# Batch 0 of k: two rows of w3 loaded ahead of it, its maximum taken by pairs of heads from PSUM, and a new order of the steps behind

## The chip, the cores and the metric

The kernel runs on one core of one Trainium2 chip. The metric is the device time of one execution in microseconds, lower is better. Each engine of the core (PE for matmuls, DVE and ACT and POOL for work on whole tiles, SP for DMA issues) takes its own instructions in the order in which the program gives them, and waits on semaphores for the others.

## The reference, cut to what matters

```python
# q, k, v: (8 batches, 8 heads, 576 tokens, 64)
q_s = exp(q - max(q, axis=-1));  q_s /= sum(q_s, axis=-1) + 1e-9     # over the 64 of a head
k_s = exp(k - max(k, axis=2));   k_s /= sum(k_s, axis=2) + 1e-9      # over the 576 tokens
kv  = einsum('bhsd,bhse->bhde', k_s, v)
x   = einsum('bhsd,bhde->bhse', q_s, kv)        # then as (8 * 576 tokens, 512)
h   = (x @ w1) * (x @ w2) @ w3                  # w1, w2: 512 x 1024, w3: 1024 x 1024
out = h @ w_out                                 # w_out: 1024 x 512, out: 4608 x 512
```

The maximum over k is taken over tokens, for each head and each of its 64 columns.

## The kernel before, in words

All work is cut into named steps. `Plan.add` registers a step with its engine and what it needs; the string `ORDER` is the order, written out by hand, in which the steps are emitted. So on each engine the steps stand in the order of `ORDER`, and a step that waits holds up all that stand behind it on that engine. A suffix (/A, /D, /P) chooses ACT, DVE or POOL where a step may run on more than one.

The steps that the opening of the kernel is made of, with their tiles in the profile:

- **Loads.** `q.0.0`, `q.0.1` and, from batch 2 on, all of q, k and v are issued by SP; all other loads (`w3.r` is row block r of w3, `wo` halves of w_out, `w1`, `w2` column blocks, `k.0.0` and `k.0.1` the two pairs of heads of batch 0, `v.0`, `k.1`, `q.1.x`, `v.1`) by POOL, in the order of `ORDER`. The load of q of batch 2 waits for the last block of w1 (`GATES`).
- **Fold of w3 and w_out into W3O.** For each row block ft: `w3t.ft` transposes it on PE into a PSUM bank (tile w3t), `w3T.ft` copies it to one of two buffers (tile aux), `pf.ft.0` and `pf.ft.1` multiply it with w_out on PE (tile pf), and `W3O.ft` scales the result out of PSUM. All `down` steps need all eight.
- **k of a batch b.** `kmx` takes the maximum over the nine blocks of tokens that lie in a partition's row (tile km); `cb` takes it across partitions and spreads it (tiles kmq, mx, mxe, cb); `ksub.b.hp` subtracts it for a pair of heads hp (tile k); `kexp.b.hp` takes the exponential (tile ek); `kv.b` multiplies with v (tile pkv) and `kv2.b` divides by the sum (tiles rc, kv). For batch 0, `kmx.0.hp` is one strided reduction for each pair of heads (`kmx_one`). For the other batches ACT first copies two blocks of all heads into PSUM (`kmi.b`, tile kmp), and DVE takes maxima of it with the other blocks, in place (`kmx_half`).
- **q of a batch.** `qmx`, `qsub`, `qexp`, `qsm`, `qeps`, `qrc`, `qn` make the softmax over a head's columns; `qt` and `qT` transpose it over PE (batch 0), `qd` by a DMA (the others).
- **x and the two layers.** `xm.b` and `xt.b` are the products of q and kv (tiles xm, xt), `xs`, `xts` scale them out of PSUM (tiles x, xtail); `up.1` and `up.0` multiply with w2 and w1 (tile pab), `bs` copies the first out (tile bsb), `ab` multiplies the two on DVE (tile ab), `down` multiplies with W3O (tile po), `os` and `st` bring the result out.
- **Sums for later chunks.** `ws` (from w1, w2) and `wt` (from W3O) are sums of weight blocks that later chunks use.

PSUM has eight banks; every step that makes a PSUM tile takes a bank that an earlier tile gave back (`w3T`, `W3O`, `xs`, `bs`, `ab` and so on give back). `zero` steps are matmuls of zeros that keep PE running at the start.

From about 80 us on (the step `up.0.2.0.1`) the order is the same in both kernels.

Of the kernel before, what the change touches and what calls it, by code (L numbers as in the profile page):

```python
# [109 lines left out]
st.0.3 qd.3.1 kmx.4.1 down.1.2 qrc.4.1 ab.2.0.4 down.1.3.0 up.0.2.0.6 up.1.2.0.7 up.0.2.0.7 qd.3.0 os.1.2/A down.1.3  # L110
bs.2.0.6/A qmx.5.0 ab.2.0.6 vc.3.0/A ksub.3.0/P kexp.3.0 st.1.2 qeps.4.0/A bs.2.0.7/A qn.4.1/P os.1.3/A qsub.5.0/P
qrc.4.0 qn.4.0/P cbt.4 cbx.4 kv.3 ab.2.0.7 qexp.5.0 down.2.0 kv2.3 xm.3.0 xs.3.0.1/A xs.3.0.0/A xm.3.1 xs.3.1.0/A xt.3
xts.3.1/A xts.3.0/A cb.4 ksub.4.1/P k.5 qmx.6.1 down.2.1 xs.3.1.1/D qsm.5.0 vc.4.1/A os.2.1/A ksub.4.0/P up.1.3.0.0
up.0.3.0.0 qmx.6.0 qsub.6.0/P bs.3.0.0/A ab.3.0.0 os.2.0/A qeps.5.0/A qrc.5.0 st.1.1 qmx.5.1 qsub.5.1/P up.1.3.0.1
up.0.3.0.1 up.1.3.0.2 up.0.3.0.2 bs.3.0.1/A qd.4.1 up.1.3.0.3 up.0.3.0.3 up.1.3.0.4 ab.3.0.1 v.5 kmi.5 kmx.5.0 kmx.5.1
cbt.5 st.2.1 kexp.4.0 vc.4.0/A kexp.4.1 kv.4 bs.3.0.2/A qsub.6.1/P kv2.4 bs.3.0.4/A up.0.3.0.4 ab.3.0.4 down.2.2
bs.3.0.3/A ab.3.0.2 qexp.5.1 qd.4.0 cbx.5 qsm.5.1 qexp.6.0 xm.4.1 xs.4.1.0/A xm.4.0 xs.4.0.1/A qn.5.0/P xs.4.0.0/A
up.1.3.0.5 ws.3.1/D up.0.3.0.5 up.1.3.0.6 up.0.3.0.6 v.6 qeps.5.1/A wt.4/D ws.4.0/D os.2.2/A wt.3/D ws.3.0/D qrc.5.1
qn.5.1/P qexp.6.1 cb.5 ksub.5.0/P bs.3.0.6/A ab.3.0.6 k.6 vc.5.0/A xs.4.1.1/A up.1.3.0.7 up.0.3.0.7 q.7 qsm.6.1
ab.3.0.3 bs.3.0.5/A vc.6.0/A up.1.4.0.0 ab.3.0.5 up.0.4.0.0 up.1.4.0.1 st.1.3 bs.3.0.7/A ksub.5.1/P up.0.4.0.1 qsm.6.0  # L120
kmi.6 bs.4.0.1/A bs.4.0.0/A kmx.6.0 st.2.0 vc.6.1/A down.2.3 qeps.6.1/A os.2.3/A qrc.6.1 kmx.6.1 up.1.4.0.2 qd.5.0
qn.6.1/P qeps.6.0/A qrc.6.0 qn.6.0/P up.0.4.0.2 ab.4.0.0 up.1.4.0.3 bs.4.0.2/A ab.4.0.2 up.0.4.0.3 up.1.4.0.4
up.0.4.0.4 cbt.6 kexp.5.0 bs.4.0.3/A vc.5.1/A qmx.7.0 qsub.7.0/P ab.4.0.3 cbx.6 up.1.4.0.5 ab.4.0.1 cb.6 up.0.4.0.5
ksub.6.1/P bs.4.0.4/A ab.4.0.4 ab.3.0.7 st.0.0 xt.4 kexp.5.1 kv.5 xts.4.0/A qexp.7.0 kv2.5 bs.4.0.5/A ab.4.0.5 dm.3.1
xts.4.1/D dm.3.2 de.3.1/A qd.5.1 xm.5.0 xm.5.1 xs.5.0.1/A xs.5.0.0/A qd.6.0 ad.3.1/D xs.5.1.0/A up.1.4.0.6 up.0.4.0.6
up.1.4.0.7 up.0.4.0.7 xs.5.1.1/A st.0.1 ksub.6.0/D kexp.6.0 ad.3.3/D bs.4.0.6/A dm.3.7 kexp.6.1 bs.4.0.7/A ws.2.1/D
ad.3.2/D dm.3.6 xd.5.3/D de.3.7/A ab.4.0.6 xt.5 ad.3.4/P qmx.7.1 ab.4.0.7 xts.5.1/D kv.6 xts.5.0/A dm.3.4 de.3.2/A
dm.3.5 de.3.4/A kv2.6 dc.3.3 qd.6.1 xm.6.1 xs.6.1.0/A qsub.7.1/P dc.3.1 xd.5.2/P xs.6.1.1/A qsm.7.0 um.5.2.1 um.5.1.1
ue.5.1.1/A ue.5.2.1/A xm.6.0 xd.5.4/D xt.6 xts.6.0/A ad.4.1/D dm.3.3 xts.6.1/A dc.3.2/A um.5.1.6 xd.5.1/D dc.3.4/D
ue.5.1.2/A k.7 xs.6.0.1/A ad.4.2/D um.5.2.6 ue.5.2.2/A ad.4.4/D um.5.1.7 ws.4.1/D um.5.2.7 ue.5.2.7/A um.5.0.7  # L130
um.5.1.5 ue.5.1.4/A ue.5.1.7/A ad.4.3/D um.5.2.2 uc.5.2.1 qeps.7.0/A um.5.0.1 xs.6.0.0/A um.5.2.4 uc.5.2.3 qrc.7.0
ue.5.0.7/A um.5.1.3 uc.5.1.4/P ab.5.1.1 ue.5.0.1/A um.5.2.5 ue.5.2.4/A um.5.1.2 uc.5.1.1 ab.5.2.0/P st.3.0 st.2.2
um.5.0.2 uc.5.0.1 um.5.0.4 um.5.0.6 ue.5.0.2/A uc.5.0.3 uc.5.2.4/P um.5.3.7 xd.6.3/P qn.7.0/P dm.4.1 kmi.7 kmx.7.0
um.5.3.1 ue.5.3.7/A um.5.1.4 uc.5.1.3 ab.5.1.0/P kmx.7.1 ue.5.3.1/A um.5.3.2 uc.5.3.1 de.4.1/A um.5.0.5 ue.5.0.4/A
uc.5.0.4/P um.5.3.6 xd.6.2/P ue.5.3.2/A dm.4.6 um.5.2.3 ab.5.2.1 um.6.0.1 qexp.7.1 qsm.7.1 cbt.7 um.5.3.5 ue.5.3.4/A
dm.4.2 xd.6.1/D dm.4.7 um.6.2.1 um.5.0.3 um.5.3.3 dc.4.1 ab.5.0.1 v.7 vc.7.1/A um.5.3.4 uc.5.3.3 uc.5.3.4/P ab.5.0.0/P
de.4.7/A dm.4.4 st.3.1 qeps.7.1/A qrc.7.1 ue.6.0.1/A ab.5.3.1 um.6.0.6 ab.5.3.0/P um.6.0.7 cbx.7 cb.7 de.4.2/A dc.4.3
xd.6.4/D ue.6.0.2/A ue.6.0.7/A ue.6.2.1/A dm.4.5 de.4.4/A dc.4.4/D um.6.0.5 ue.6.0.4/A uc.6.0.4/D st.4.1 um.6.1.1
ue.6.1.1/A um.6.2.7 ue.6.2.7/A dm.4.3 dc.4.2/A um.6.3.1 ue.6.3.1/A um.6.0.4 um.6.3.7 ue.6.3.7/A um.6.0.2 ksub.7.1/D
ksub.7.0/D qd.7.0 qn.7.1/P kexp.7.1 um.6.1.6 um.6.3.6 um.6.2.6 ue.6.2.2/A uc.6.0.3 uc.6.0.1 ab.6.0.0/P um.6.3.4  # L140
vc.7.0/A um.6.2.4 uc.6.2.3 um.6.0.3 ab.6.0.1 um.6.2.2 uc.6.2.1 um.6.1.2 uc.6.1.1 um.6.1.7 um.6.3.2 uc.6.3.1 ab.6.2.0/P
um.6.2.5 ue.6.3.2/A um.6.3.5 uc.6.3.3 kexp.7.0 ue.6.2.4/A ad.5.1/D uc.6.2.4/D dm.5.1 kv.7 ue.6.1.2/A ad.5.2/D
ue.6.3.4/A uc.6.3.4/P um.6.1.5 um.6.2.3 kv2.7 st.4.0 ue.6.1.7/A um.6.1.4 de.5.1/A uc.6.1.3 ab.6.2.1 dm.5.2 um.6.3.3
# [1039 lines left out]
```

## Time and profile before

| what | value |
|---|---|
| median of 3 runs | 227.33 us (227.28 to 227.34) |
| the profiled execution | 227.57 us, its span 225.8 us |
| PE busy | 219.3 us (97%) |
| DVE busy | 203.9 us (90%) |
| ACT busy | 161.6 us (72%) |
| POOL busy | 141.1 us (62%) |
| read from and written to HBM | 38.80 MB, 9.44 MB |

The span is the time from the program's first to its last instruction; the execution's own time is somewhat longer. A row of the timeline has the start, the duration, the engine, the line, the operation, the tiles (out<-in) with their shapes, how many instructions the row merges, and in brackets the engine's idle time ahead of it with what ended it. The ends of matmuls are modelled, so a short wait of PE can stand in a row as a longer duration.

### The profile page before, as it was taken

The numbers are of one execution on the slowest core, as the hardware profiler recorded it, in microseconds if no ns is written. First come the engines' busy times: TensorE is split into PE (matmuls) and PEld (weight loads), VectorE is DVE, ScalarE is ACT, GpSimd is POOL, SyncE is SP. The second block draws the span as 40 slices with busy tenths as digits, with TensorE's granted clock in tenths as the row PEclk, the third lists the DMA queues.
The fourth block names the chain that finished last, engine by engine and source line by source line (L and its number), as shares of the span: only waits on it lengthen the run. The fifth ranks groups of instructions, "written<-read, shape, count | busy, mean of one in ns | idle before, by whom it ended". The sixth has DMA issues, their size and how long they took to land.

```text
span 225.8 us, 5662 instructions
## 1 busy us (share of the span) xinstructions
PE 219.3 (97%) x2250; PEld 150.6 (67%) x2250; DVE 203.9 (90%) x363; ACT 161.6 (72%) x280; POOL 141.1 (62%) x96
## 2 busy tenths in 40 slices
...
GB/s 222 214 273 248 294 227 251 367 387 300 277 276 369 388 324 357 187 312 280 385 164 296 22 134 212 128 221 96 32 200 64 3 107 34 3 124 157 89 145 139
DMA packets 38042, 46.89 MB, mean 208 GB/s; under 512 B 18048, under 2 KB 21504, under 8 KB 38016
## 3 DMA queue, kind: packets, MB, share of 16 engines
...
q8 instruction: 17, 0.28, 0.5%
...
HBM read 38.80 MB, written 9.44 MB: 214 GB/s over the span
## 4 chain that ended last, share of the span: by engine, by line
PE 67%; DMA 20%; DVE 8%; ACT 2%; POOL 1%; issue 1%; POOLq 0%; ACTq 0%; SPq 0%; DVEq 0%
PE pab L809 19%; PE uA L904 12%; PE dA L945 8%; DMA w1sb<-in_moe_w_dram 8%; PE uB L904 6%; PE po L842 6%; DMA w<-in_moe_w_dram 5%; DMA wosb<-in_moe_w_out_dram 5%; PE dB L945 4%; DMA q<-in_q_dram 3%; PE uC L904 3%; PE po L857 3%; PE dC L945 2%; DVE qm L547 2%; PE pkv L501 2%; DVE qr L579 2%
## 5 line engine op out<-in xcount | busy, mean ns | idle before, releaser
L809 PE MATMUL pab<-x,w2sb 128*128 128x256 f16 (+1 forms) x224 | 40.6, 318 | 0.0
L809 PE MATMUL pab<-x,w1sb 128*128 128x256 f16 (+1 forms) x224 | 40.6, 318 | 0.0
L597 POOL TENSOR_TENSOR en<-eq,qr 128x1024 f16<-128x1024 f16 (+1 forms) x14 | 29.7, 2126 | 8.3 <-DVE k L475 4.3
L809 PEld LDWEIGHTS <-w2sb 128*128 128x128 f16 x224 | 21.6, 98 | 13.4 <-issue 1.0
L809 PEld LDWEIGHTS <-w1sb 128*128 128x128 f16 x224 | 21.7, 98 | 13.0 <-issue 0.2
L553 POOL TENSOR_TENSOR q<-q,qm 128x1280 f32<-128x1280 f32 (+1 forms) x13 | 27.7, 2143 | 2.2 <-DVE qm L547 1.8
L475 POOL TENSOR_TENSOR k<-k,cb 128x1152 f32<-128x1152 f32 x10 | 26.2, 2626 | 2.5 <-DVE k L475 2.5
L904 PEld LDWEIGHTS <-w 128*128 128x128 f16 x256 | 25.0, 98 | 3.3
L834 DVE TENSOR_TENSOR ab<-pab,bsb 128x512 f16<-128x512 f32 x40 | 25.9, 672 | 0.2
L275 ACT CAST bsb<-pab 128x512 f16<-128x512 f32 x40 | 23.2, 594 | 3.8 <-PE pab L809 3.6
L561 ACT ACTIVATE eq<-q 128x1024 f16<-128x1024 f32 (+2 forms) x16 | 18.7, 1169 | 8.2 <-DVE q L553 7.6
L547 DVE TENSOR_REDUCE qm<-q 128x16 f32<-128x1024 f32 (+2 forms) x16 | 21.2, 1333 | 3.7 <-DMA q<-in_q_dram 3.7
L842 PE MATMUL po<-W3O,ab 128*128 128x512 f16 x96 | 22.7, 380 | 0.0
L579 DVE TENSOR_REDUCE qr<-eq 128x16 f32<-128x1024 f16 (+2 forms) x16 | 21.4, 1339 | 0.0
L483 ACT ACTIVATE ek<-k 128x1152 f16<-128x1152 f32 x16 | 18.8, 1172 | 3.3 <-DVE k L475 2.4
L279 ACT ACTIVATE x<-xm 128x512 f16<-128x512 f32 x30 | 16.4, 605 | 3.6 <-PE xm L649 1.9
L904 PE MATMUL uA<-v,w 128*128 128x256 f16 x128 | 17.9, 273 | 0.0
L275 ACT COPY v<-uA 128x512 f32<-128x512 f32 x24 | 14.1, 601 | 4.8 <-PE uA L904 4.3
L945 PEld LDWEIGHTS <-k 128*128 128x128 f16 x160 | 15.5, 98 | 2.1
L883 POOL TENSOR_TENSOR k<-ab,k 128x1024 f16<-128x1024 f16 x3 | 6.4, 2130 | 16.4 <-DVE bsb L883 10.0
L275 ACT CAST v<-v 128x1152 f16<-128x1152 f32 x14 | 16.3, 1170 | 0.0
L398 PE MATMUL pf<-wosb,aux 128*128 128x512 f16 x64 | 15.6, 379 | 0.4 <-DMA wosb<-in_moe_w_out_dram 0.4
(140 smaller groups left out, 464.7 us busy)
## 6 DMA issues: line engine op xcount, KB each, us to landing
...
```

The costliest lines, as they stand in the source:

```text
L275: return [(nc.scalar.copy if eng == "ACT" else engine[eng].tensor_copy)(out=out, in_=in_)]
L475: return [engine[eng].tensor_tensor(out=kb[:, two(hp), :, :], in0=kb[:, two(hp), :, :], in1=st["cb", b][:, two(hp), None, :].broadcast_to( ...
L483: nc.scalar.activation(out=st["ek", b][:, hp, :, :].rearrange("p j (i d) -> p i j d", i=2), in_=kb[:, two(hp), :, :], func=AF.Exp)
L547: dve.tensor_reduce(out=st["qm", b][:, hs, j], in_=qb[:, hs, j, :], axis=AX.X, op=ALU.max, **({"negate": True} if (b, p) in FEXP else {}))
L553: return [engine[eng].tensor_tensor(out=qb[:, hs, j, :], in0=qb[:, hs, j, :], in1=st["qm", b][:, hs, j, None].broadcast_to([P, nh, n, D]), ...
L579: dve.tensor_reduce(out=st["qr", b][(slice(None), *part(p))], in_=st["eq", b, p], axis=AX.X, op=ALU.add)
L597: return [engine[eng].tensor_tensor(out=st["en", b][:, j, hs, :].rearrange("p j h d -> p h j d"), in0=st["eq", b, p], in1=st["qr", b][:, h ...
L809: nc.tensor.matmul(st["p", one, c, sub, u][:, a * (t1 - t0):(a + 1) * (t1 - t0)], lhsT=w[:, ct, fb * P:(fb + 1) * P], rhs=x()[:, ct, t0:t1 ...
L834: dve.tensor_tensor(out=st["ab", c][:, nf * u:nf * u + nf, t0:t1], in0=cut(st["p", 0, c, sub, u]), in1=cut(st["bsb", c, sub, u]), op=ALU.mult)
L842: nc.tensor.matmul(st["po", c, tb], lhsT=st["ab", c][:, ft, tb * P:(tb + 1) * P], rhs=W3O[:, ft, :], start=(ft == 0), stop=(ft == N_FT - 1))
L904: nc.tensor.matmul(t[:, u, :], lhsT=w[:, k0 + kk, fb * P:(fb + 1) * P], rhs=r[:, kk, :], start=(p in (1, 2, 7) and u == 0 and kk == 0), st ...
L945: nc.tensor.matmul(t[:, i, :], lhsT=l[:, f, i * P:(i + 1) * P], rhs=r[:, f, :], start=(p in (1, 2, 7) and i == 0 and f == 0), stop=(i == 1 ...
```

## The change

`KM = [0]` gives batch 0 two new steps for each pair of heads hp in place of the strided reduction. `kmi.0.hp` (ACT) copies the first two blocks of tokens of the pair into a PSUM bank, as 2 x 128 columns; `kmx.0.hp` (DVE) takes the maximum of it with blocks 2 and 3, 4 and 5, 6 and 7 in place (three instructions of 256 columns), and then with block 8 and of the two halves (two of 128 columns). `ALOAD` is empty and so does nothing.

In `ORDER`, `w3.7` and `w3.5` are loaded ahead of `k.0.1` and `k.0.0`; the first 33 steps are the same, and from there to `up.0.2.0.1` the steps stand in a new order, thirteen of them on another engine (`qsub.1.0` and `ws.1.1` from DVE to POOL, `wt.2` from POOL to DVE, and moves between ACT and DVE).

```diff
-qt.0.0.4 qT.0.0.4/A wo.1 pf.3.1 zero.6/1 qsm.0.1 w3.6 w3t.6 qeps.0.1/A qrc.0.1 qT.0.0.0/D qn.0.1/D pf.4.1 W3O.4/D w3.0
-w3t.0 W3O.3/D w3T.6/A pf.6.0 qt.0.1.0 w3T.0/A qT.0.1.0/A qt.0.1.4 pf.6.1 qT.0.1.4/A W3O.6/A pf.0.0 k.0.1 kmx.0.1 k.0.0
-w3.7 w3t.7 w3T.7/A pf.0.1 w3.5 w3t.5 pf.7.0 pf.7.1 w3T.5/A pf.5.0 w3.1 w3.2 v.0 k.1 kmx.0.0 cb.0 ksub.0.0/D kexp.0.0
-w3t.1 w3T.1/D W3O.7/A ksub.0.1/D pf.5.1 w2.1 w2.0 w1.0 q.1.0 W3O.5/D w2.2 w3t.2 pf.1.0 kexp.0.1 pf.1.1 W3O.1/D w1.1
-kv.0.0 kv.0 kv2.0 w3T.2/A pf.2.0 kmi.1 kmx.1.0 xm.0.1 xt.0 xs.0.1.1/A xs.0.1.0/A xts.0.0/A xts.0.1/D pf.2.1 W3O.2/A
-xm.0.0 xs.0.0.1/A xs.0.0.0/A q.1.1 up.1.0.1.0 W3O.0/A wt.1/P up.1.0.1.1 up.1.0.0.1 up.1.0.0.0 bs.0.1.1/A up.0.0.0.0
-bs.0.0.1/A kmx.1.1 cb.1 bs.0.0.0/A qmx.1.0 up.0.0.0.1 up.0.0.1.0 qsub.1.0/D ksub.1.1/D ab.0.0.1 qexp.1.0 qsm.1.0
-up.1.0.0.3 bs.0.0.3/A up.0.0.1.1 ab.0.1.1 q.2 v.1 kexp.1.1 k.2 qeps.1.0/A ksub.1.0/P up.1.0.1.2 kexp.1.0 up.1.0.0.2
-qrc.1.0 bs.0.0.2/A qn.1.0/P up.0.0.0.3 up.0.0.0.2 ab.0.0.0 qmx.1.1 qd.1.0 qsub.1.1/P bs.0.1.0/A ab.0.0.3 up.1.0.1.3
-up.0.0.1.3 ab.0.0.2 k.3 ab.0.1.0 bs.0.1.3/A ab.0.1.3 ws.1.1/D up.0.0.1.2 bs.0.1.2/A ab.0.1.2 down.0.0.0 qmx.2.0
-down.0.0 down.0.1.0 down.0.1 vc.1.1/A vc.1.0/A qexp.1.1 qsm.1.1 qeps.1.1/A ws.1.0/P qsub.2.0/P kv.1.0 kv.1 q.3 kv2.1
-qexp.2.0 down.0.2.0 down.0.2 qrc.1.1 xm.1.0 qn.1.1/P qd.1.1 qmx.2.1 down.0.3.0 down.0.3 qsm.2.0 qeps.2.0/D kmi.2
-kmx.2.0 qsub.2.1/P xs.1.0.0/A v.2 xs.1.0.1/A up.1.1.0.0 bs.1.0.0/A os.0.2/A st.0.2 up.0.1.0.0 os.0.3/A qrc.2.0
-qn.2.0/P wt.2/P up.1.1.0.1 up.0.1.0.1 bs.1.0.1/A qexp.2.1 kmx.2.1 up.1.1.0.2 cb.2 bs.1.0.2/A ksub.2.0/P up.0.1.0.2
-up.1.1.0.3 os.0.0/A os.0.1/A xm.1.1 xs.1.1.1/A qsm.2.1 xs.1.1.0/D ab.1.0.1 qeps.2.1/A qrc.2.1 ab.1.0.0 bs.1.0.3/A
-up.0.1.0.3 up.1.1.1.0 up.0.1.1.0 up.1.1.1.1 qmx.3.1 up.0.1.1.1 ab.1.0.3 ab.1.0.2 bs.1.1.0/A up.1.1.1.2 up.0.1.1.2
-up.1.1.1.3 qn.2.1/P kexp.2.0 down.1.0.0 down.1.0 kmi.3 kmx.3.0 bs.1.1.1/A ab.1.1.1 vc.2.0/A qd.2.0 xt.1 bs.1.1.2/A
-ksub.2.1/P vc.2.1/A kmx.3.1 cbt.3 kexp.2.1 qsub.3.1/P xts.1.0/A ab.1.1.2 xts.1.1/A q.4 qexp.3.1 ws.2.0/P ab.1.1.0 kv.2
-kv2.2 down.1.1.0 down.1.1 qd.2.1 xm.2.1 qmx.3.0 qsub.3.0/P os.1.0/A bs.1.1.3/A xs.2.1.1/A qmx.4.1 qsub.4.1/P xm.2.0
-xs.2.0.1/A xt.2 qsm.3.1 xs.2.0.0/A xs.2.1.0/A cbx.3 xts.2.1/A v.3 down.1.2.0 up.0.1.1.3 up.1.2.0.0 bs.2.0.0/A qmx.4.0
-xts.2.0/D up.0.2.0.0 up.1.2.0.1 qsub.4.0/P up.0.2.0.1 up.1.2.0.2 k.4 v.4 qexp.3.0 cb.3 ksub.3.1/P qsm.3.0 os.1.1/A
...
+qt.0.0.4 qT.0.0.4/A wo.1 pf.3.1 w3.6 w3t.6 qT.0.0.0/A w3.0 w3.7 w3T.6/A pf.4.1 w3t.0 w3T.0/A w3.5 k.0.1 k.0.0 w3.1
+w3.2 kmi.0.1 qsm.0.1 qeps.0.1/D pf.6.0 qrc.0.1 qn.0.1/D pf.6.1 zero.6/1 W3O.3/D W3O.6/D qt.0.1.0 w3t.5 w3T.5/A w3t.7
+kmi.0.0 pf.0.0 pf.0.1 v.0 pf.5.0 kmx.0.1 qT.0.1.0/A w3T.7/A pf.5.1 W3O.5/A pf.7.0 kmx.0.0 cb.0 ksub.0.0/D w3t.2
+ksub.0.1/D w3T.2/A pf.7.1 kexp.0.0 qt.0.1.4 qT.0.1.4/D kexp.0.1 W3O.4/A pf.2.0 pf.2.1 w3t.1 w3T.1/D k.1 kv.0.0 kv.0
+kv2.0 W3O.0/A w2.1 w2.0 w1.0 q.1.0 w2.2 w1.1 q.2 pf.1.0 kmi.1 W3O.2/A W3O.7/A xm.0.0 xs.0.0.0/A xs.0.0.1/D xm.0.1
+xs.0.1.1/A q.1.1 xt.0 xts.0.1/D pf.1.1 up.1.0.0.1 up.1.0.0.0 kmx.1.0 xs.0.1.0/A up.1.0.1.0 bs.0.1.0/A v.1 xts.0.0/A
+up.1.0.1.1 up.0.0.1.1 up.0.0.1.0 W3O.1/D wt.1/P up.0.0.0.0 bs.0.1.1/A kmx.1.1 qmx.1.0 qsub.1.0/P bs.0.0.0/A up.1.0.0.2
+qexp.1.0 cb.1 bs.0.0.1/A ksub.1.1/D up.1.0.1.2 bs.0.0.2/A up.1.0.1.3 qsm.1.0 qeps.1.0/A bs.0.1.3/A ab.0.1.0 up.0.0.0.1
+kexp.1.1 ksub.1.0/P kexp.1.0 up.1.0.0.3 bs.0.0.3/A up.0.0.0.3 qrc.1.0 qn.1.0/P ab.0.1.1 qmx.1.1 ab.0.0.1 ab.0.0.0
+up.0.0.1.3 ab.0.1.3 up.0.0.0.2 ab.0.0.2 up.0.0.1.2 ab.0.0.3 k.2 bs.0.1.2/A ab.0.1.2 qmx.2.0 vc.1.1/A down.0.0.0
+down.0.0 vc.1.0/A down.0.1.0 qsub.1.1/P qexp.1.1 qsm.1.1 qeps.1.1/A qd.1.0 kv.1.0 kv.1 kv2.1 down.0.1 os.0.1/A v.2
+ws.1.1/P down.0.2.0 down.0.2 kmi.2 qsub.2.0/P qexp.2.0 xm.1.0 xs.1.0.0/A qrc.1.1 qmx.2.1 qn.1.1/P xs.1.0.1/A kmx.2.0
+qsm.2.0 q.3 kmx.2.1 os.0.0/A os.0.2/A qeps.2.0/A down.0.3.0 ws.1.0/P qrc.2.0 down.0.3 os.0.3/A up.1.1.0.0 up.0.1.0.0
+bs.1.0.0/A up.1.1.0.1 up.0.1.0.1 bs.1.0.1/A ab.1.0.0 up.1.1.0.2 up.0.1.0.2 up.1.1.0.3 qsub.2.1/P qexp.2.1 bs.1.0.2/A
+cb.2 bs.1.0.3/A qd.1.1 xm.1.1 xs.1.1.0/A xs.1.1.1/A xt.1 ab.1.0.1 qsm.2.1 qn.2.0/P up.0.1.0.3 down.1.0.0 qeps.2.1/A
+xts.1.0/A qmx.3.0 qrc.2.1 vc.2.1/A ab.1.0.2 k.3 ksub.2.0/P kmi.3 kexp.2.0 up.1.1.1.0 ab.1.0.3 qmx.3.1 up.0.1.1.0
+qn.2.1/P q.4 up.1.1.1.1 bs.1.1.1/A kmx.3.0 bs.1.1.0/A up.0.1.1.1 ab.1.1.0 kmx.3.1 vc.2.0/A qmx.4.0 st.0.2 xts.1.1/A
+up.1.1.1.2 ksub.2.1/P kexp.2.1 qd.2.0 up.0.1.1.2 up.1.1.1.3 bs.1.1.2/A ab.1.1.2 bs.1.1.3/A qsub.3.1/P qexp.3.1
+down.1.0 os.1.0/A kv.2 kv2.2 ab.1.1.1 qmx.4.1 down.1.1.0 down.1.1 qd.2.1 xm.2.0 xs.2.0.0/A xm.2.1 xs.2.1.1/A cbt.3
+xs.2.0.1/A xs.2.1.0/A xt.2 qsub.3.0/P xts.2.0/D qsub.4.0/P xts.2.1/D qsm.3.1 qsub.4.1/P down.1.2.0 cbx.3 up.0.1.1.3
+up.1.2.0.0 bs.2.0.0/A v.3 wt.2/D up.0.2.0.0 ws.2.0/P up.1.2.0.1 up.0.2.0.1 up.1.2.0.2 k.4 v.4 qexp.3.0 cb.3 ksub.3.1/P
...
@@
+    KM = [0]
+    ALOAD = []
@@
-            load((n, b), "SP")
+            load((n, b), "ACT" if (n, b) in ALOAD else "SP")
@@
+        def kmi_one(hp):
+            st["kmp", b, hp] = bank([P, 2, 2, D], F32, "kmp")
+            nc.scalar.copy(out=st["kmp", b, hp], in_=kb[:, two(hp), 0:2, :].rearrange("p h j d -> p j h d"))
+
+        def kmx_max(hp):
+            t = st["kmp", b, hp]
+            top = lambda out, in0, in1: dve.tensor_tensor(out=out, in0=in0, in1=in1, op=ALU.max)
+            for j in (2, 4, 6):
+                top(t, t, kb[:, two(hp), j:j + 2, :].rearrange("p h j d -> p j h d"))
+            if ("km", b) not in st:
+                st["km", b] = work.tile([P, HH, D], F32, tag="km", name="km")
+            m = st["km", b][:, two(hp), :]
+            top(m, t[:, 0], kb[:, two(hp), 8, :])
+            top(m, t[:, 1], m)
@@
             for hp in hps:
-                A(("kmx", b, hp), "DVE", lambda hp=hp: kmx_one(hp), [("k", b, hp)])
+                if b in KM:
+                    A(("kmi", b, hp), "ACT", lambda hp=hp: kmi_one(hp), [("k", b, hp)], takes="ps", kind="kmi1")
+                    A(("kmx", b, hp), "DVE", lambda hp=hp: kmx_max(hp), [("kmi", b, hp)], gives=[("kmi", b, hp)],
+                      kind="kmq")
+                else:
+                    A(("kmx", b, hp), "DVE", lambda hp=hp: kmx_one(hp), [("k", b, hp)])
```

113 lines of the change are left out of this document (57 added, 56 removed).

## The prediction

> **What bounds the kernel now.** I read the page first, then the chain, then the timelines of PE, POOL, DVE and ACT over the opening, since the order changes only up to about 80 us.
>
> ```profile
> PE 219.3 (97%) x2250; PEld 150.6 (67%) x2250; DVE 203.9 (90%) x363; ACT 161.6 (72%) x280; POOL 141.1 (62%) x96
> PE 67%; DMA 20%; DVE 8%; ACT 2%; POOL 1%; issue 1%; POOLq 0%; ACTq 0%; SPq 0%; DVEq 0%
> ```
>
> PE is busy 97% of the span, but the chain that ended last is PE for only 67%. The chain in order of time (start, us, what) says where the rest lies:
>
> ```profile
> 25.05 16.98 DMA w1sb<-in_moe_w_dram
> 42.10 7.75 DMA q<-in_q_dram
> 49.88 1.22 DVE qm L547
> ...
> 71.26 1.07 ACT ek L483
> 72.85 1.83 PE po L842 x8
> ```
>
> Up to 72.3 us the chain runs through the last weight load, q of batch 2 gated behind it, DVE and ACT; from 72.85 on it is PE alone. So two things must be followed: when the dense work of PE begins, and how much PE still waits between there and 72.85. The PE timeline (start, us; in brackets the idle time and who ended it):
>
> ```profile
> 22.63 0.71 PE L388 MATMUL w3t<-ident,w 128*128 128x128 f16 x8 [0.85 <-DMA w<-in_moe_w_dram]
> ...
> 30.15 0.48 PE L501 MATMUL pkv<-v,ek 64*64 64x64 f16 x36
> 30.56 0.38 PE L510 MATMUL pkv<-ones,ek 64*128 64x1 f16 x18
> ...
> 31.84 0.56 PE L649 MATMUL xm<-qT,kv 64*64 64x256 f16 x8
> 32.12 0.33 PE L649 MATMUL xt<-qT,kv 64*64 64x64 f16 x8
> 32.38 1.04 PE L398 MATMUL pf<-wosb,aux 128*128 128x512 f16 x4
> 33.35 0.41 PE L649 MATMUL xm<-qT,kv 64*64 64x256 f16 x8
> 33.70 3.67 PE L809 MATMUL pab<-x,w2sb 128*128 128x256 f16 x32
> ...
> 51.23 0.78 PE L501 MATMUL pkv<-v,ek 64*64 64x65 f16 x72
> ...
> 62.42 0.41 PE L649 MATMUL xm<-qT,kv 64*64 64x256 f16 x8 [0.27 <-DMA qT<-en]
> ...
> 71.67 1.18 PE L501 MATMUL pkv<-v,ek 64*64 64x65 f16 x72
> ```
>
> PE waits for row 5 of w3 at 22.63 (w3t.5). From there it is packed with folds up to 33.70, where the first up begins. After that it loses 0.27 at xm.1.1 (62.42) and, hidden in a busy time, 1.18 - 0.78 = 0.40 at kv.2 (71.67), which waits for kexp.2.1, the ACT piece of the chain. Those 0.67 us are all that a later up can hide in, and, with the start of up, all that there is to gain. In both orders every fold stands ahead of the first up, so PE has the same work left at that point, and the question is how far its start moves.
>
> **Part 1: two rows of w3 ahead of k.0.** POOL issues a load when the one eight places earlier has landed, so its waits tell the landings:
>
> ```profile
> 16.33 0.76 POOL L358 DMA_DIRECT2D k<-in_k_dram  x1 [0.49 <-DMA w<-in_moe_w_dram]
> 17.82 0.74 POOL L358 DMA_DIRECT2D w2sb<-in_moe_w_dram  x1 [0.73 <-DMA k<-in_k_dram]
> 19.30 0.74 POOL L358 DMA_DIRECT2D w2sb<-in_moe_w_dram  x1 [0.73 <-DMA k<-in_k_dram]
> 20.43 0.74 POOL L358 DMA_DIRECT2D w1sb<-in_moe_w_dram  x1 [0.39 <-DMA w<-in_moe_w_dram]
> 22.86 0.76 POOL L358 DMA_DIRECT2D q<-in_q_dram  x1 [1.70 <-DMA w<-in_moe_w_dram]
> ```
>
> These rows follow the landings of w3.0, k.0.1, k.0.0, w3.7 and w3.5 (the last by 22.63, when PE takes it). The four loads after w3.0 take from 16.3 to 22.6 whatever their order; the change makes k.0.0 the last of them instead of the second. k.0.0 then lands at 22.6 rather than 19.3. Even spacing by the same rows (two rows at 1.13, two halves at 1.5) would give 21.6; I take 22.6, since w3.5 in that last place did take until then. w3.7 and w3.5 land near 17.5 and 18.7, so PE no longer waits for them. The bytes ahead of every later load are the same, and so is the landing of w1.1 that gates q.2.
>
> **Part 2: the maximum of k.0 by pairs.** Two strided reductions go; for each pair there come an ACT copy of 256 elements into PSUM, three maxima of 256 and two of 128.
>
> ```profile
> 17.67 4.27 DVE L429 TENSOR_REDUCE km<-k 128x128 f32<-128x1152 f32 x2
> 21.98 0.45 DVE L468 STREAM_TRANSPOSE kmq<-km 128x256 f32<-128x256 f32 x1
> ...
> 24.28 1.36 DVE L475 TENSOR_TENSOR k<-k,cb 128x1152 f32<-128x1152 f32 x1
> ...
> 27.15 1.35 DVE L475 TENSOR_TENSOR k<-k,cb 128x1152 f32<-128x1152 f32 x1
> ...
> 34.10 0.42 DVE L439 TENSOR_TENSOR km<-kmp,k 128x256 f32<-128x256 f32 x1
> ```
>
> For 128 elements, the row of the view that groups instructions by shape (busy us, mean ns):
>
> ```profile
> L531 DVE TENSOR_TENSOR kv<-pkv,rc 128x128 f16<-128x128 f32 x2 | 0.5, 284 | 0.0
> ```
>
> A reduction takes 4.27 / 2 = 2.14; a pair will take 3 x 0.42 + 2 x 0.284 = 1.83, with small gaps 1.9. [...]
>
> The copy on ACT lies between 0.28 and 0.59:
>
> ```profile
> 23.43 1.01 ACT L275 COPY aux<-w3t 128x1024 f16<-128x1024 f16 x1 [1.42 <-PE w3t L388]
> ...
> 28.53 1.17 ACT L483 ACTIVATE ek<-k 128x1152 f16<-128x1152 f32 x1 [1.20 <-DVE k L475]
> ...
> 30.64 0.59 ACT L435 COPY kmp<-k 128x512 f32<-128x512 f32 x1
> 32.44 1.09 ACT L279 ACTIVATE x<-xm 128x512 f16<-128x512 f32 x2 [1.21 <-PE xt L649]
> 33.41 0.28 ACT L279 ACTIVATE xtail<-xt 128x128 f16<-128x128 f32 x1
> ```
>
> I take 0.38, nearer to the 128-element row. The two copies make ACT wait for landings of k.0; behind them queue w3T.5, qT.0.1.0, w3T.7, W3O.5 and w3T.2, and PE's pf.5 and pf.7 wait for those. w3T.7 ends about 24.6: the copy until 23.0 (part 3), then 0.6 and 1.01. The folds left then, four pf halves at 0.97 (32.38 to 33.35) and w3t.2 and w3t.1 at 0.7, 5.3 us, end near 29.9, ahead of kv.0 at 31.05 below, so this costs nothing; the cover is 1.1 us, and past it every us on ACT is a us on PE.
>
> **Part 3: the path to up.** k.0.0 lands 22.6; copy to 23.0; kmx.0.0 to 24.9; cb.0 as in the rows, 24.28 - 21.98 = 2.30, to 27.2; ksub.0.1 begins 1.3 later, 28.5; kexp.0.1 begins 28.53 - 27.15 = 1.38 after it, 29.9, and ends at 31.05 (28.53 + 1.17 = 29.70 before). kv.0 takes 0.8 (30.15 to 30.94), to 31.9; kv2.0 takes 31.84 - 30.94 = 0.9, so xm.0.0 starts at 32.8, against 31.84 for the first xm before: **+1.0**.
>
> Then ACT. Its order after kexp.0.1 is W3O.4, W3O.0, kmi.1, W3O.2, W3O.7, xs.0.0.0; the two scalings in the 1.09 row give 0.55 each, so W3O.7 ends at 31.05 + 5 x 0.55 = 33.8. Of the eight PSUM banks, those free when xt.0 asks for two were held for W3O.2, W3O.7 and the two halves of xm.0.0; the first in line are the W3O's, so xt.0 stands until 33.8 although its data are there at 33.4. xt.0 0.26 and pf.1.1 0.97 (32.12 to 32.38 to 33.35) follow: up starts at **35.1, +1.4**. With other banks it is 34.65 (+0.95); with even landing as well DVE gains 0.6 (the first pair ends at 22.4 then): +0.35. Upwards, k.0.1 late by a us too, or 0.59 copies, add 0.4: +1.8.
>
> **Part 4: after up.** DVE reaches its own queue later by the same 1.0, yet hands work away: qsub.1.0 and ws.1.1 go to POOL, wt.2 comes back.
>
> ```profile
> 38.49 1.23 DVE L553 TENSOR_TENSOR q<-q,qm 128x1024 f32<-128x1024 f32 x1
> ...
> 47.90 0.69 DVE L1125 TENSOR_TENSOR w<-w2sb 128x1024 f16<-128x1024 f16 x1
> ...
> 49.88 1.22 DVE L547 TENSOR_REDUCE qm<-q 128x16 f32<-128x1024 f32 x1 [0.69 <-DMA q<-in_q_dram]
> ```
>
> ```profile
> 51.18 1.91 POOL L553 TENSOR_TENSOR q<-q,qm 128x1024 f32<-128x1024 f32 x1 [0.38 <-DVE qm L547]
> ...
> 60.53 2.13 POOL L1131 TENSOR_TENSOR aux<-W3O,aux 128x1024 f16<-128x1024 f16 x1
> ```
>
> That is 1.23 + 0.69 = 1.9 off DVE by 50 us, and there it also idled 0.69 for q.2. POOL gets 1.91 and about 2.13 and loses 2.13; qsub.1.0 falls where it stood waiting for DVE. So the data for xm.1.1 and kexp.2.1 should come about when they came before, PE arrives about 1.4 later, and both waits, 0.67, close. v.1 is now issued ahead of wt.1 on POOL, but its bytes stand behind q.1.1 in the same queue; v.2 and k.3 change places on SP, which neither user (70 us) needs so early. I cost these at nothing; if the cover of v.2 or k.3 fails, ACT's casts or kmi.3 are late next, up to 1 us.
>
> **Sum.** +1.4 - 0.67 = +0.7. The profiled execution took 227.57, 1.8 around its span of 225.8; it would become 228.3. It stands 0.24 over the median of the runs, 227.33, so the median becomes 228.1.
>
> **Rivals.** A measurement here can tell about 0.2%, 0.45 us, from no change.
> - *Balance, no change:* the loads land evenly, or xt.0 gets other banks, up moves by 0.35 to 0.95, and the two waits swallow it: 227.0 to 227.6. For it: the waits are there. Against: w3.5 in the last place landed late. Chance 0.20.
> - *Faster:* in the order before, PE was packed from 22.63 by folds of rows that came late, and kv.0 at 30.15 began 0.45 after its exponential ended at 29.70. If both halves of k.0 land 1.4 earlier than in my sum, k.0.0 at 21.2, ACT's W3O's stay off the path and xs.0.0.0 and xs.0.0.1 run side by side, up begins at 33.4: -0.3 - 0.67, about 226.4. It decides at kexp.0.1: it must end by 29.7. That the loads land in another order than issued, so that k.0 isn't put back, ends here too; POOL's rows above speak against that. Chance 0.18.
> - *Slower still:* DVE, late by 1.0 and held by xs.0.0.1 and xts.0.1, reaches ab.0 late; down.0.0 needs ab.0.0.3 and stands 0.3 to 1.0: 228.5 to 229.2. For it: before, DVE finished these with little to spare. Chance 0.14.
> - *Forecast:* 227.8 to 228.4, chance 0.48.
>
> **How the numbers follow.** Slower by over 0.2% (above 227.78) is 0.48 + 0.14 = 0.62, within 0.20, faster 0.18. The likeliest case gives 228.1. The range runs from 226.8, inside the faster case, to 229.2, leaving some 0.15 out.
>
> **What would show it.** Right: w3t.5 and w3t.7 without a wait near 19 to 20; kmi.0.0 waiting for DMA to about 22.6; kexp.0.1 at about 29.9; xt.0 or xs.0.0.0 after W3O.7; the first pab at 35.1; no idle at xm.1.1 and 72 pkv in about 0.8 at kv.2. Wrong: the first pab at or before 33.9, kexp.0.1 ending by 29.7, or a new PE wait over 0.3 between 45 and 73.

## The result and the profile after

| | median of the runs | range | runs |
|---|---|---|---|
| before | 227.34 us | 227.25 to 228.31 | 9 |
| after | 228.62 us | 228.02 to 230.99 | 9 |

The ratio is 1.0063 (95% interval 1.0045 to 1.0080): slower, by about 1.3 us. The profiled execution of after took 228.45 us, its span is 226.6 us, 0.8 over that of before.

The page of after, the busy times and the chain that ended last:

```profile
PE 218.7 (96%) x2250; PEld 150.9 (67%) x2250; DVE 201.7 (89%) x370; ACT 162.0 (71%) x282; POOL 143.0 (63%) x97
...
PE 85%; DMA 9%; DVE 3%; ACT 1%; issue 1%; POOL 1%; POOLq 0%; ACTq 0%
```

The same chain in order of time (start, us, what):

```profile
9.09 13.65 DMA k<-in_k_dram
27.59 2.64 DVE k L493 x2
32.25 0.97 PE pf L401 x4
```

Before, the chain left the loads, DVE and ACT for PE at 72.85. Now it does so at 32.25: k.0.0, the two subtractions, kexp.0.1, then PE. The waits at xm.1.1 and kv.2 have left it.

The PE timeline of after:

```profile
30.20 0.48 PE L519 MATMUL pkv<-v,ek 64*64 64x64 f16 x36 [0.44 <-ACT ek L501]
...
31.46 0.48 PE L519 MATMUL pkv<-v,ek 64*64 64x64 f16 x36 [0.48 <-ACT ek L501]
...
33.15 0.78 PE L667 MATMUL xm<-qT,kv 64*64 64x256 f16 x16
33.66 0.52 PE L667 MATMUL xt<-qT,kv 64*64 64x64 f16 x8
...
34.98 3.66 PE L832 MATMUL pab<-x,w2sb 128*128 128x256 f16 x32
...
63.34 0.41 PE L667 MATMUL xm<-qT,kv 64*64 64x256 f16 x8
...
72.56 0.78 PE L519 MATMUL pkv<-v,ek 64*64 64x65 f16 x72
...
106.84 0.78 PE L519 MATMUL pkv<-v,ek 64*64 64x65 f16 x72
...
110.67 0.63 PE L667 MATMUL xm<-qT,kv 64*64 64x512 f16 x8 [0.35 <-issue]
```

Two rows of the PE timeline of before, which the prediction didn't need, for the last two of these:

```profile
106.40 0.78 PE L501 MATMUL pkv<-v,ek 64*64 64x65 f16 x72
...
109.80 0.63 PE L649 MATMUL xm<-qT,kv 64*64 64x512 f16 x8
```

Take the difference of equal steps: PE is 1.28 us late at the first up (34.98 against 33.70), 0.92 at xm.1.1, 0.49 at the end of kv.2 (73.34 against 72.85), 0.44 at kv.4 (106.84 against 106.40). So far it is what the prediction said. Then, in a stretch where both orders are the same, PE loses another 0.43 at xm.4 and ends 0.87 late. The profile puts that wait down to "issue". What comes last there is `qd.4.0`, a DMA transpose of q (the transposes write tile qT). The DMA view of after, from 101.9 to 104 us (tile, engine, count, median us from issue to landing):

```profile
qT<-en SPq DMA_TRANSPOSE x1, 8.4
```

It was issued at 102.16 (below) and so landed at 110.6, and xm.4 starts at 110.67. The cause is to be looked for in what SP does earlier. The SP timeline of before, then of after (a row with x2 runs from the start of the first issue to the end of the second, with any pause of SP between them):

```profile
61.26 1.73 SPq L631 DMA_TRANSPOSE qT<-en  x1
63.09 0.53 SPq L358 DMA_DIRECT2D q<-in_q_dram  x1
67.56 1.26 SPq L631 DMA_TRANSPOSE qT<-en  x1
68.92 0.71 SPq L358 DMA_DIRECT2D v<-in_v_dram  x1
...
86.91 4.63 SPq L631 DMA_TRANSPOSE qT<-en  x2
...
101.32 1.43 SPq L631 DMA_TRANSPOSE qT<-en  x1
```

```profile
62.01 0.37 SPq L361 DMA_DIRECT2D q<-in_q_dram  x1
...
63.73 7.01 SPq L649 DMA_TRANSPOSE qT<-en  x2
70.84 0.54 SPq L361 DMA_DIRECT2D v<-in_v_dram  x1
...
87.06 6.56 SPq L649 DMA_TRANSPOSE qT<-en  x2
...
102.16 3.36 SPq L649 DMA_TRANSPOSE qT<-en  x1
```

In before, q.4 stood between qd.2.0 and qd.2.1; in after it stands ahead of both. Taken one by one, the two transposes of after hold SP for 3.36 us from 63.73 and for 2.77 us from 67.97; those of before held it for 1.73 and 1.26. So SP is free only at 70.74, and v.3 is issued 1.9 us later. The issues behind v.3 hardly move: k.4 and v.4 come 0.15 us earlier than in before, q.5, q.6 and the transposes of batch 3 0.15 to 0.23 later. What moves is a landing: q.6, issued at 84.02, takes 8.8 us, against 5.9 for the one issued at 83.79 in before. And from 87 on the transposes of batch 3 hold SP for 3.62 and 2.84 us instead of 1.47 and 2.76.

The DMA view from 88 to 94 us, in 40 slices of 0.15 us (busy share of the 16 DMA engines in tenths; GB/s), of before and then of after:

```profile
DMA  9999999999999995700000599999999999998899
GB/s 369 384 384 384 364 384 425 386 389 386 306 391 203 164 61 32 12 7 9 10 10 9 109 283 295 290 283 274 292 287 295 288 288 274 164 218 178 260 369 246
```

```profile
DMA  9999998899999999992392919111111500079999
GB/s 338 307 369 338 369 338 314 335 352 408 342 304 362 251 230 119 111 113 92 102 77 72 87 56 50 58 58 43 39 48 46 24 27 27 14 116 276 292 288 285
```

Loads run at over 300 GB/s, then the rate falls, then the transposes run at some 270 to 295. The stretch under 150 GB/s between them lasts 9 slices (1.35 us) in before and 21 (3.15 us) in after, most of it with a tenth or two of the DMA engines busy: a remainder of the loads trails (q.6 lands at 92.8), and the transposes begin only behind it.

### The profile page after: what moved, and what is told of

Same layout as the page of the kernel before. It is cut to its first block, busy times and chain, and to the rows that moved or that the text cites. A ratio compares the mean times of both kernels' runs of the same rounds, so it can differ in the third digit from the quotient of the medians.

```text
span 226.6 us, 5669 instructions
## 1 busy us (share of the span) xinstructions
PE 218.7 (96%) x2250; PEld 150.9 (67%) x2250; DVE 201.7 (89%) x370; ACT 162.0 (71%) x282; POOL 143.0 (63%) x97
## 4 chain that ended last, share of the span: by engine, by line
PE 85%; DMA 9%; DVE 3%; ACT 1%; issue 1%; POOL 1%; POOLq 0%; ACTq 0%
PE pab L832 31%; PE uA L927 12%; PE po L865 9%; PE dA L968 8%; PE uB L927 6%; DMA k<-in_k_dram 6%; PE dB L968 4%; PE uC L927 3%; PE po L880 3%; DMA w<-in_moe_w_dram 3%; PE pkv L519 2%; PE xm L667 2%; PE dC L968 2%; DVE k L493 1%; PE pf L401 1%
## 5 line engine op out<-in xcount | busy, mean ns | idle before, releaser
L571 POOL TENSOR_TENSOR q<-q,qm 128x1024 f32<-128x1024 f32 (+1 forms) x14 | 29.6, 2127 | 1.1 <-DVE qm L565 1.1
L278 ACT CAST bsb<-pab 128x512 f16<-128x512 f32 x40 | 22.8, 591 | 5.5 <-PE pab L832 5.0
```

Source lines behind the costliest of these rows:

```text
L278: return [(nc.scalar.copy if eng == "ACT" else engine[eng].tensor_copy)(out=out, in_=in_)]
L571: return [engine[eng].tensor_tensor(out=qb[:, hs, j, :], in0=qb[:, hs, j, :], in1=st["qm", b][:, hs, j, None].broadcast_to([P, nh, n, D]), ...
```

## The experiments

Theory at first: the opening, up 1.28 later less the hidden waits, sets the end. Rivals: the new order behind up costs by itself; the pairs cost. From e5 on the theory is SP's order. Each ratio is to before, measured beside the run (its medians there were 227.39 to 227.67 us).

**e1, after again**, unchanged, for the spread.

```diff
 (no edit)
```

> The changed kernel once more, on the chip of the next three. In its first profile the first up began at 34.98 us (33.70 before), PE was 0.89 us behind at kv.2 and 0.48 behind after it, and lost another 0.42 ahead of xm of batch 4 at 110 us, so it ended 0.86 behind. Theory (the late half of k.0 sets the start of up, and all but the two old waits stays): first up within 0.1 us of 34.98 again and 0.3 to 0.5 behind after kv.2. The 0.42 at 110 us may be there or not: if it is of the order it comes again at the same step, if it is the DMA queue's timing it moves. Ratio to before 1.004 to 1.008.

Measured: 228.84 us, ratio 1.0064 (1.0035 to 1.0093). In its profile (a run of 230.88 us) the first up is at 35.81, 0.83 later than in the other profile of the same kernel: the landings of the opening vary by that much, and "within 0.1 us of 34.98" missed. xm.4 waits again, 1.08 us.

**e2, the reductions back**, the new order kept.

```diff
-    KM = [0]
+    KM = []
...
-w3.2 kmi.0.1 qsm.0.1 ... w3t.7 kmi.0.0 pf.0.0
+w3.2 qsm.0.1 ... w3t.7 pf.0.0
```

> The changed kernel with the two strided reductions in place of the ACT copies and the maxima by pairs; all else stands. Theory (behind a late landing the pair costs more than it saves): the copy (0.38 and a hop) and the five maxima took 22.75 to 25.25, 2.50 us, where one reduction takes 2.14, so the first up comes at about 34.6 instead of 34.98, and the time falls by 0.1 to 0.4 us; ACT has no wait for k.0. Rival (pairs save DVE time, as they were meant to): 2 x (2.14 - 2.02) on DVE is lost, the first up comes at 35.1 to 35.3 and the time rises by 0.1 to 0.3.

Measured: 228.72 us, ratio 1.0053 (1.0037 to 1.0069); the first up is at 34.84, 0.14 earlier than in after. So the pairs bring nothing to the path, their cost can't be told from nothing, and after's loss isn't theirs.

**e3, the loads back**: w3.7 and w3.5 behind k.0, with the folds that use them.

```diff
-... w3.0 w3.7 w3T.6/A pf.4.1 w3t.0 w3T.0/A w3.5 k.0.1 k.0.0 w3.1 ...
+... w3.0 w3T.6/A pf.4.1 w3t.0 w3T.0/A k.0.1 k.0.0 w3.7 w3.5 w3.1 ...
-... w3t.5 w3T.5/A w3t.7 kmi.0.0 pf.0.0 pf.0.1 v.0 pf.5.0 kmx.0.1 qT.0.1.0/A w3T.7/A pf.5.1 W3O.5/A pf.7.0 kmx.0.0 ...
+... kmi.0.0 pf.0.0 pf.0.1 w3t.7 v.0 kmx.0.1 qT.0.1.0/A w3T.7/A w3t.5 w3T.5/A pf.7.0 pf.7.1 pf.5.0 pf.5.1 W3O.5/A kmx.0.0 ...
```

> The changed kernel with w3.7 and w3.5 loaded behind k.0.1 and k.0.0 again, and the folds of these two rows put where the rows then arrive (w3t.7, pf.7, then w3t.5, pf.5); pairs and the order behind stay. Theory: k.0.0 lands at 19.0, kexp.0.1 ends near 28.2 and is off the path; PE is packed from the landing of w3.5 at 22.6: three folds of 1.73, three transposes of rows at 0.5, q's transposes 0.3, kv 1.6, the halves of pf.1 and xm, xt 2.6: the first up at 33.9 to 34.2, and 0 to 0.2 us behind before after kv.2; ratio to before 1.000 to 1.003. Rival (the order behind is what costs): the first up may move, but the time stays at 1.006.

Measured: 228.94 us, ratio 1.0059 (1.0041 to 1.0076). Its PE timeline:

```profile
34.41 3.66 PE L831 MATMUL pab<-x,w2sb 128*128 128x256 f16 x32
...
110.27 0.63 PE L666 MATMUL xm<-qT,kv 64*64 64x512 f16 x8 [0.55 <-issue]
```

Up is 0.57 earlier than in after, yet xm.4, where PE now waits 0.55, starts only 0.40 earlier, and the median isn't better. The time doesn't follow the opening.

**e4, before's opening, after's order behind it** (and the reductions).

```diff
-(the steps of after up to pf.1.1)
+(the steps of before up to q.1.1, the last ahead of up.1.0.1.0)
 (behind it: the steps of after that are left, in after's order)
```

> All steps up to the first up in the order of before (reductions, k.0 ahead of rows 7 and 5), all steps behind in the order of the changed kernel, with the first four up in the order of before. Theory: the first up at 33.7 as before; the order behind is neutral: PE reaches kv.2 about 1.2 us earlier than in the changed kernel and waits there for kexp.2.1 (72.2 us in both), so it is within 0.15 us of before after kv.2; ratio 0.998 to 1.002. Rival (the order behind costs): ratio 1.004 to 1.007. A third view (the order behind gains, and the opening hid it): under 0.998.

Measured: 228.54 us, ratio 1.0039 (1.0021 to 1.0056). Its PE timeline, then its SP timeline:

```profile
32.97 3.67 PE L831 MATMUL pab<-x,w2sb 128*128 128x256 f16 x32
...
110.77 0.63 PE L666 MATMUL xm<-qT,kv 64*64 64x512 f16 x8 [1.10 <-DVE qr L596]
```

```profile
63.47 7.02 SPq L648 DMA_TRANSPOSE qT<-en  x2
70.58 0.54 SPq L360 DMA_DIRECT2D v<-in_v_dram  x1
```

Up starts 0.73 earlier than in before, and the kernel is slower than before: PE waits 1.10 at xm.4. The row names DVE, but qd.4.0, issued at 102.30, landed 8.4 us later, at 110.7, just ahead of xm.4. That the opening alone sets the end falls here.

**e5, before with SP's order of after.**

```diff
 order on SP
-qd.1.0 k.3 q.3 qd.1.1 v.2 st.0.2 qd.2.0 q.4 qd.2.1 v.3
+qd.1.0 v.2 q.3 qd.1.1 k.3 q.4 st.0.2 qd.2.0 qd.2.1 v.3
```

> The kernel before, with only the SP queue in the order of the kernel after: k.3 and v.2 change places, q.4 and st.0.2 stand ahead of qd.2.0, so that qd.2.0 and qd.2.1 follow each other on SP. No other engine's order changes. Theory SP (the two transposes in a row hold SP, the loads and the transposes behind come later, and xm.4 waits for qd.4.0): ratio to before 1.003 to 1.006; the first up as before, 33.7; qd.2.0 and qd.2.1 take some 7 us of SP instead of 3; PE waits 0.6 to 1.2 us at xm.4, near 110. Theory opening (the later first up sets the end): ratio 0.999 to 1.001, no wait at xm.4. Theory middle (the new order of the other engines' steps between 45 and 75 us sets it): also 0.999 to 1.001.

Measured: 227.93 us (227.24 to 228.74), ratio 1.0018 (1.0000 to 1.0036), below what was expected. The row of the two transposes is 8.28 us long (4.62 and 2.91 one by one), yet in the profile, which is of the shortest run (227.24), the row of those of batch 3 is 4.68 long and xm.4 doesn't wait. Whether the longer runs had the wait isn't shown.

**e8, before with q.4 alone moved.**

```diff
 order on SP
-v.2 st.0.2 qd.2.0 q.4 qd.2.1 v.3
+v.2 q.4 st.0.2 qd.2.0 qd.2.1 v.3
```

> The kernel before, with only q.4 and st.0.2 set ahead of qd.2.0 on SP; k.3 and v.2 stay. Theory SP in the form that the transposes in a row cost it: as e5, ratio 1.003 to 1.006, qd.2.0 and qd.2.1 some 7 us on SP. In the form that v.2 ahead of k.3 costs it: 0.999 to 1.001, and e5 alone is slower.

Measured: 227.92 us, ratio 1.0025 (1.0009 to 1.0041). Its SP timeline and its PE timeline:

```profile
62.23 8.26 SPq L631 DMA_TRANSPOSE qT<-en  x2
...
86.95 6.71 SPq L631 DMA_TRANSPOSE qT<-en  x2
```

```profile
110.39 0.63 PE L649 MATMUL xm<-qT,kv 64*64 64x512 f16 x8 [0.47 <-issue]
```

One load moved past one transpose (and a store) in the kernel before makes both signs of after: a row of 6.71 us on SP at 87, and a wait at xm.4. Its size, 0.25%, is under the 0.3 expected.

**e6 and e7, after and e4 with SP's order of before.**

```diff
 order on SP (e6 and e7; qmx.4.0 goes with q.4)
-qd.1.0 v.2 q.3 qd.1.1 k.3 q.4 st.0.2 qd.2.0 qd.2.1 v.3
+qd.1.0 k.3 q.3 qd.1.1 v.2 st.0.2 qd.2.0 q.4 qd.2.1 v.3
```

> The kernel after, with only the SP queue in the order of the kernel before: k.3 where v.2 stood, v.2 behind qd.1.1, q.4 between qd.2.0 and qd.2.1. Theory SP: first up at 35.0 as in after, PE then late by 0.3 to 0.5 from kv.2 to the end, no wait over 0.2 at xm.4: ratio 1.001 to 1.002. Theory opening: 1.003 to 1.006 as in after, since nothing of the opening changes. Theory middle: also 1.003 to 1.006, with a wait at xm.4 or elsewhere behind 75 us.

> As e4 (before's opening, after's order behind the first up), with the SP queue in before's order. Theory SP: the lead that e4 had after kv.2 (0.2 us ahead of before) is kept to the end: ratio 0.998 to 1.001. Theory middle: 1.003 to 1.005 as e4. If it comes out under 0.998, the order behind up is by itself better than before's.

Measured: e6 228.50 us, 1.0043 (1.0025 to 1.0062); e7 228.53 us, 1.0045 (1.0027 to 1.0062). Both miss the theory of SP's order and lie where its rivals, the opening and the new order of the other engines, had put them. The first reason is a new wait. The ACT and the PE timeline of e7:

```profile
66.58 1.15 ACT L277 CAST v<-v 128x1152 f16<-128x1152 f32 x1 [2.55 <-DMA v<-in_v_dram]
```

```profile
69.84 1.03 PE L831 MATMUL pab<-x,w1sb 128*128 128x256 f16 x8 [1.03 <-ACT bsb L277]
```

When v.2 stands behind qd.1.1, it lands 2.55 us after ACT, in after's order, is ready to cast it. ACT stands 2.55 us, the casts of up behind it are late, and PE loses 1.03 (in e6 1.90 and 0.52). So v.2 has to stay where the new order has it, and q.4 must be put back alone. But the wait for v.2 isn't all. The SP and the PE timeline of e7 further on:

```profile
87.42 6.40 SPq L648 DMA_TRANSPOSE qT<-en  x2
...
110.72 0.63 PE L666 MATMUL xm<-qT,kv 64*64 64x512 f16 x8 [0.46 <-issue]
```

In e7 q.4 stands between the two transposes, these hold SP for 1.32 and 1.27 us, and v.3 is issued at 68.60, earlier than in before. Both signs are there all the same (in e6 a row of 5.98 us, and a wait of 0.29 at xm.4). So q.4's place isn't the only thing that brings them about. In both runs the loads from k.4 on and the transposes of batch 3 are issued 0.2 to 1.0 us later than in before; whether that is the reason isn't shown.

**e9, after with q.6 behind qd.3.0**, so that the transposes meet fewer loads.

```diff
 order on SP
-q.5 st.1.0 q.6 st.0.3 qd.3.1 qd.3.0 st.1.2
+q.5 st.1.0 st.0.3 qd.3.1 qd.3.0 q.6 st.1.2
```

> The kernel after, with the load of q.6 moved on SP from ahead of st.0.3, qd.3.1 and qd.3.0 to behind them (its first user, qmx.6.1, comes some 10 us later). Theory backlog (the transposes qd.3.1 and qd.3.0 meet loads that are still trailing in the DMA queue, which then holds everything behind them some 3 us, up to qd.4.0, for which PE stands at xm.4): without q.6 ahead of them the transposes take under 5 us of SP, qd.4.0 lands before 109.5, no wait over 0.15 us at xm.4; PE keeps its lag of 0.3 to 0.5 from the opening: ratio 1.001 to 1.003. Theory back-to-back transposes (what counts is qd.2.0 and qd.2.1 in a row, and all loads late from there): xm.4 still waits, ratio 1.004 to 1.007. Theory opening: 1.004 to 1.007 as after.

Measured: 228.22 us, ratio 1.0026 (1.0012 to 1.0040), within the range of the theory; the row of the transposes of batch 3 is 4.17 us long, and xm.4 starts without a wait. But the profiled run had a late opening (up at 35.77), PE reached xm.4 only at 111.16, and qd.4.0 still landed near 110.5 (issued 102.55, 8.0 to landing): that part of the expectation failed, the missing wait proves little, and the gain is only partly explained.

**e10, after with v.3 ahead of qd.2.0.**

```diff
 order on SP
-st.0.2 qd.2.0 qd.2.1 v.3 k.4
+st.0.2 v.3 qd.2.0 qd.2.1 k.4
```

> The kernel after, with the load of v.3 set ahead of qd.2.0 on SP instead of behind qd.2.1, so that the DMA queue is not left empty while the two transposes are issued. Theory backlog: v.3 lands 2 to 4 us earlier than 77.1, k.4, v.4 and q.5 near 80.0, 83.0 and 86.4 as in before, q.6 lands near 90 instead of 92.8, and xm.4 does not wait: ratio 1.001 to 1.003. If the loads come earlier and qd.4.0 still lands after 110, the backlog of k.4 to q.5 isn't the cause: 1.004 to 1.007.

Measured: 230.64 us, ratio 1.0137 (1.0111 to 1.0163): above both ranges, by 1.5 us. Its SP and its PE timeline:

```profile
65.19 9.35 SPq L648 DMA_TRANSPOSE qT<-en  x2
```

```profile
78.12 0.63 PE L666 MATMUL xm<-qT,kv 64*64 64x512 f16 x8 [2.12 <-DMA qT<-en]
```

With a load more in flight ahead of them the transposes hold SP for 5.39 and 3.88 us, and the next user of one, xm.2, waits 2.12. This profiled run had the late opening too (up at 35.82), but e1's, with up at 35.81, began xm.2 at 75.92 without a wait. So an empty queue isn't what costs the time; as far as this run goes, loads directly ahead of transposes are. At xm.4 there is no wait here.

**e11, the opening alone**: after up to its first up, then before's order on every engine (the first four steps of up stand as in after).

```diff
 (the steps of after up to pf.1.1)
-(the steps that are left, in after's order)
+(the steps that are left, in before's order)
```

> The kernel after up to its first up (rows of w3 ahead of k.0, the maximum by pairs, the folds' order), then the steps of the kernel before in their old order on every engine, SP's too. Forecast's own sum: up 1.3 later, less the two hidden waits of 0.67: 0.3 to 0.7 late from kv.2 to the end, ratio 1.002 to 1.003. Theory backlog: since the loads hang on PE's progress, 0.3 to 0.7 late at kv.2 is enough to turn xm.4's landing late in most runs: 1.003 to 1.006, with PE waiting at xm.4. Theory SP order alone: 1.001 to 1.003, no wait at xm.4.

Measured: 230.84 us, ratio 1.0142 (1.0123 to 1.0161), far outside all three. Its PE timeline:

```profile
34.86 3.66 PE L831 MATMUL pab<-x,w2sb 128*128 128x256 f16 x32
...
45.09 1.91 PE L831 MATMUL pab<-x,w1sb 128*128 128x256 f16 x16 [0.46 <-ACT bsb L277]
...
59.05 0.93 PE L831 MATMUL pab<-x,w2sb 128*128 128x256 f16 x7 [0.22 <-ACT x L281]
```

Up is 1.16 later than in before; the step of the second row is 1.78 later (43.31 in before), and the step that the third row goes on with, begun at 58.56, is 2.68 later (55.88 in before). Behind before's order the late opening grows; behind after's order it shrinks.

**e12, e4 with q.4 alone back between the transposes.**

```diff
 order on SP (qmx.4.0 goes with q.4)
-k.3 q.4 st.0.2 qd.2.0 qd.2.1 v.3
+k.3 st.0.2 qd.2.0 q.4 qd.2.1 v.3
```

> As e4 (before's opening, after's order behind the first up), with v.2 and k.3 in after's order on SP, and only q.4 moved back between qd.2.0 and qd.2.1. qmx.4.0 goes with it; its place among DVE's own steps stays. Theory SP (the two transposes in a row cost the time): the two take some 3 us of SP instead of 6.4, qd.3.1 under 2 us instead of 4.0, qd.4.0 lands before 109.5, xm.4 does not wait, and PE keeps the 0.2 us that e4 was ahead at kv.2: ratio 0.998 to 1.000, which would beat the kernel before if at the lower end. If xm.4 still waits for a landing near 110.5 with q.4 back, the transposes in a row are not what decides, and any small shift of the loads does: 1.002 to 1.005.

Measured: 227.14 us (226.91 to 228.09, 12 runs), ratio 0.9993 (0.9978 to 1.0008), against 1.0039 (1.0021 to 1.0056) for e4: the two intervals don't meet. Its SP timeline, the DMA view from 88 to 94, and the PE timeline:

```profile
67.12 1.26 SPq L648 DMA_TRANSPOSE qT<-en  x1
68.48 0.54 SPq L360 DMA_DIRECT2D v<-in_v_dram  x1
...
86.43 4.57 SPq L648 DMA_TRANSPOSE qT<-en  x2
```

```profile
GB/s 384 376 428 403 411 348 365 441 314 236 172 135 82 55 44 32 14 10 19 266 295 287 290 271 290 287 294 283 295 332 191 164 191 191 369 246 191 43 154 92
```

```profile
109.20 0.63 PE L666 MATMUL xm<-qT,kv 64*64 64x512 f16 x8
```

v.3 is issued 2.1 us earlier than in e4, the slack stretch is back at 8 slices (1.2 us), and xm.4 starts at 109.20 without a wait, 1.57 earlier than in e4. (The profile is of a run of 226.96 us; three of the twelve took 227.9 to 228.1, and whether those waited isn't shown.) Between these two kernels one load's place on SP is worth 0.46%, 1.0 us. That the new order of the other engines costs by itself falls here, behind before's opening. Against before e12 can't be told from no change.

**All profiles together.** Where q.6 lands within 7 us of its issue (before 5.9, e5 6.9, e10 5.8, e12 6.4), xm.4 doesn't wait. Where it takes 8.3 to 9.3 us (after, e1 to e4, e6 to e8), PE waits at xm.4 for 0.29 to 1.10 us, and xm.4 starts 0.1 us behind the landing of qd.4.0. In e11 q.6 takes 8.9, but PE comes to xm.4 only at 112.79 and doesn't wait; in e9 q.6 stands elsewhere. So the late landing of q.6 and the wait at xm.4 go together. What makes it late isn't settled: q.4's place does so in e8 and e4, but it isn't enough in the profile of e5, and in e6, e7 and e11 it happens without.

## Why the prediction came out as it did

The time lay in the range of 226.8 to 229.2, the sign was right, and the mechanism was right as far as it was followed, to 73 us. What ended last it didn't have. The median is 0.5 above the likeliest 228.1 and outside the forecast's own 227.8 to 228.4. The span grew by 0.8, near the +0.7 of the sum, but that is in part luck: 0.44 of it is the opening, less the hidden waits, at kv.4, and 0.43 a wait at xm.4 that the sum didn't have.

**Landings (Part 1): right.** The ACT timeline of after, first the copy that waits for k.0.0:

```profile
22.82 0.38 ACT L442 COPY kmp<-k 128x256 f32<-128x256 f32 x1 [1.28 <-DMA k<-in_k_dram]
...
28.98 2.43 ACT L501 ACTIVATE ek<-k 128x1152 f16<-128x1152 f32 x2 [1.67 <-DVE k L493]
...
32.79 1.09 ACT L282 ACTIVATE W3O<-pf 128x512 f16<-128x512 f32 x2
```

k.0.0 came at 22.8 (22.6 said), a copy took 0.38, as said, and the transposes of rows 5 and 7 of w3 ran from 19.05 without a wait.

**The pair (Part 2): a little long.** On DVE of after:

```profile
23.23 1.36 DVE L446 TENSOR_TENSOR kmp<-kmp,k 128x256 f32<-128x256 f32 x3 [0.58 <-ACT kmp L442]
...
24.96 0.29 DVE L446 TENSOR_TENSOR km<-kmp,km 128x128 f32<-128x128 f32 x1
```

From 23.23 to 25.25 it is 2.02, against 1.9 said and 2.14 for a reduction. Measured, a pair gains 0.12 on DVE, and with the copy of 0.38 on ACT ahead loses 0.26. By e2 neither reaches the end.

**The path to up (Part 3): right.** kexp.0.1 ended at 31.41 instead of 31.05, and xm.0.0 began at 33.15 instead of 32.8. The second scaling of the 32.79 row, W3O.7, ended at 33.88 (33.8 said). The row of xt.0 hides a wait for it: two of its eight matmuls start at 33.66 and 33.76, the other six only from 33.93 on, so the row is 0.52 long instead of 0.33 in before. The bank thus held xt.0 as said, but for some 0.2 instead of 0.4, since the late xm.0.0 had taken the rest. The two errors cancel, and up came at 34.98 (35.1 said). On PE a wait of 1.03 at pf.7 stayed under cover, since PE waits for ek at 30.20 and 31.46 anyway.

**After up (Part 4): the hidden waits right, the SP moves wrong.** The 0.67 did close: the lag fell from 1.28 to 0.49. That the new order would make up for the late opening was right for a stronger reason than given: e11 shows the same opening costing 3.2 us behind the old order. But "I cost these at nothing" failed, and by an edit that it didn't list: it weighed v.1, v.2 and k.3 and left out q.4, which passes qd.2.0 on SP. That this load's place costs time is shown by e8 and by e4 against e12; that it is what costs it in after is argued from them. And the argument ended at 73 us since "the order changes only up to about 80": in after the late landings go on into steps whose order is the same, q.6 in 8.8 us instead of 5.9, and then qd.4.0 at 110.6 with PE waiting for it. That the users of v.2 come only at 70 us was wrong too: in after ACT casts v.2 at 65.25, and e7 shows the price of a late one, the "up to 1 us" of that sentence.

**The rivals.** Balance and faster didn't come. The median, 228.62, lies in the 228.5 to 229.2 of "slower still", but PE didn't stand at down.0.0. Its place was taken by a wait at xm.4.

How much of after's 0.63% is q.4's place and how much the opening isn't split cleanly: behind before's opening q.4's place is the 0.46% between e4 and e12; after with q.4 alone back wasn't run. Nor can the two simply be added: e6 and e7 show the wait at xm.4 with q.4 back and the other steps late.
